# First block of a two-layer attention and MLP kernel: x and the values' weights first, constant work for TensorE meanwhile, values ahead of the folding

## The chip, the cores and the metric

The kernel runs on one core of a Trainium2 chip. The metric is device time in microseconds (us); the runs before the change gave a median of 1380.86. A core has TensorE (PE in the profile, its weight loads PEld), VectorE (DVE), ScalarE (ACT), GpSimd (POOL) and SyncE (SP), which here issues the transfers.

## The reference

Four sub-layers, each added to its input: linear attention with a learned feature map, an MLP with Mish, and both once more with the same weights. S = 2048 rows, D = 640, H = 32 heads of 20, F = 1536, all float32.

```python
def _A_ref(x, wqkv, w_phi, wo):
    qkv = (x @ wqkv).reshape(B, S, 3, H, Dh).transpose(2, 0, 3, 1, 4)
    q, k, v = qkv[0], qkv[1], qkv[2]
    pq = jnp.einsum("bhsd,hdf->bhsf", q, w_phi)
    pk = jnp.einsum("bhsd,hdf->bhsf", k, w_phi)
    phi_q = concatenate([softmax(pq), softmax(-pq)], axis=-1)     # phi_k alike
    kv = jnp.einsum("bhsf,bhsd->bhfd", phi_k, v)
    z = jnp.einsum("bhsf->bhf", phi_k)
    num = jnp.einsum("bhqf,bhfd->bhqd", phi_q, kv)
    den = jnp.einsum("bhqf,bhf->bhq", phi_q, z)[..., None] + 1e-6
    return (num / den).transpose(0, 2, 1, 3).reshape(B, S, D) @ wo
...
x = x + _A_ref(_layernorm(x), wqkv, w_phi, wo)
x = x + _B_ref(_layernorm(x), w1, b1, w2)      # dense, Mish, dense
x = x + _A_ref(_layernorm(x), wqkv, w_phi, wo)
x = x + _B_ref(_layernorm(x), w1, b1, w2)
```

## The kernel before

The rows are worked in eight blocks of 256, each of two tiles of 128 rows (tile t of block b is rows 2p+t). Every large product is made of three float32r matmuls, high by high, high by low and low by high parts; a high part (`r1h`, `r2h`, `xth`) is a ScalarE copy, the low part (`r1l`, `r2l`, `xtl`) is VectorE's difference from it.

The feature map's matrix is folded into the query and key weights on the chip: `fold_phi` (L227) multiplies the transposed weights (`raw`, from `wqk_t`) by a block-diagonal matrix (`bd`, from `phi_bd`). It goes by ten groups, five row groups k by two column halves c, each of three float32 matmuls (six in the trace) and emptied by ScalarE (L242) and VectorE (L243). There is one folding for the queries (into `r2`) and one for the keys (into the first 640 columns of `r1`); the values' weights, split by L127 and L128, are in the next 640 columns of `r1`.

A block's x is fetched (L384), its mean and variance come from VectorE (L250, L252) and a little GpSimd work (L259, L260), the scalings are L262, ScalarE writes the normalized rows `xn` (L113, L116), TensorE transposes them (L280) and the parts are split (ScalarE L116, VectorE L286). Per tile there are then three projections (`project_half`, L344): keys, values, queries, 30 matmuls each. Keys and queries go through `features`: a ScalarE copy out of PSUM, VectorE reductions (L368), subtractions (L369 on VectorE or GpSimd, L371), an exponential, a sum (L377), a reciprocal (L378) and a GpSimd product (L379). Keys are then multiplied with the values (L416); queries are transposed on VectorE (L424) and written out.

The start, in `attend_first`: SyncE asks in written order for half of `bd`, three of the queries' raw tiles, block 0's x, the rest of `bd` and raw, and after the folding for the values' weights and the keys' raw rows. Everything else is placed on the engines by a scheduler that works from its own estimates (`tc.block(schedule_with_timeline_sim=True)`); `tc.manual_schedule` keeps the written order for the engines it names, and `tc.issue_after` holds an instruction behind another. Within a block the projections have a written order (`order`): block 0 has v0, q0, v1, k0, q1, k1, block 1 has k0, q0, k1, v0, q1, v1, the later ones k0, k1, v0, v1, q0, q1. PSUM has two double tiles `mm` and four single tiles `one`.

Of the kernel before, what the change touches and what calls it, by code (L numbers as in the profile page):

```python
# [1 line left out]

# [6 lines left out]
F32 = mybir.dt.float32  # L9
F32R = mybir.dt.float32r  # L10
AF = mybir.ActivationFunctionType
# [5 lines left out]
P = 128  # L17
# [24 lines left out]
def kernel(  # L42
# [25 lines left out]
    def one_tile():  # L68
        return psum.tile([P, 512], F32, tag="one", name="one", bufs=4)
# [13 lines left out]

    ident = const.tile([P, P], F32, name="ident")
    make_identity(nc, ident)
    b1s = const.tile([P, KF], F32, name="b1s")
    neg_half = const.tile([P, BT], F32, name="neg_half")
    nc.vector.memset(neg_half, -0.5)
# [16 lines left out]
    x1_d = dram.tile([S, D], F32, name="x1_d")  # L105
    x2_d = dram.tile([S, D], F32, name="x2_d")

    last_act = [None]

    def act(*args, **kw):  # L110

        if last_act[0] is None:
            ins = nc.scalar.activation(*args, **kw)  # L113
        else:
            with tc.issue_after(last_act[0]):
                ins = nc.scalar.activation(*args, **kw)  # L116
        last_act[0] = ins.ins


    def v_tile():  # L120
        return work.tile([P, VW], F32, tag="v", name="v", bufs=2)

    def split(hi, lo, src, stage):

        st = stage()[:, :D]
        nc.sync.dma_start(st, src)
        nc.scalar.activation(hi, st, AF.Copy)  # L127
        nc.vector.tensor_tensor(lo, st, hi.bitcast(F32), op=ALU.subtract)  # L128

# [25 lines left out]
    def r1_pair(k):  # L155
        return tuple(wts.tile([P, F], F32R, tag=f"r1{s}{k}", name=f"r1{s}{k}") for s in "hl")
# [4 lines left out]
    def r2_pair(j):  # L161
# [2 lines left out]
            return w[:, 0], w[:, 1]  # L164
        return tuple(wts.tile([P, D], F32R, tag=f"r2{s}{j}", name=f"r2{s}{j}") for s in "hl")

    def load_v_weights():

        ws = [r1_pair(k) for k in range(KD)]
        for k in range(KD):  # L170
            split(ws[k][0][:, D:2 * D], ws[k][1][:, D:2 * D], wv[k * P:(k + 1) * P, :],
                  (row_tile, row_tile, v_tile, v_tile, big_tile)[k])
        return ws

    def load_q_weights():
# [36 lines left out]
    def load_raw(which, ts=range(6)):  # L212

        raw = []
        for t in ts:
            rows = 120 if t < 5 else 40
            if t < 5:
                r = wts.tile([P, D], F32, tag=f"r2{'hl'[which]}{5 + t}", name=f"raw{which}{t}")
            else:
                r = r2_wide(10 + which, F32)[:, 0]  # L220

            n = P if t < 5 else rows
            nc.sync.dma_start(r[:n], wqk_t[which * D + t * 120:which * D + t * 120 + n, :])
            raw.append((r, rows))
        return raw

    def fold_phi(ws, bd, raw):  # L227

        pss = {}
        for k, c in ((0, 0), (1, 0), (2, 0), (3, 0), (0, 1), (1, 1), (2, 1), (3, 1), (4, 0), (4, 1)):  # L230
            if c == 0:
                mm = None if k % 2 else mm_tile()
                pss[k] = [one_tile(), one_tile()] if k % 2 else [mm[:, 0], mm[:, 1]]
            ps = pss[k][c]
            for t in range(3 * c, 3 * c + 3):
                r, rows = raw[t]
                nc.tensor.matmul(ps[:, (t % 3) * 120:(t % 3) * 120 + rows],  # L237
                                 r[:rows, k * P:(k + 1) * P], bd[:rows, t, :rows],
                                 start=True, stop=True)
            n0, n1 = (0, 360) if c == 0 else (360, D)  # L240
            hi, lo = ws[k][0][:, n0:n1], ws[k][1][:, n0:n1]
            nc.scalar.activation(hi, ps[:, :n1 - n0], AF.Copy)  # L242
            nc.vector.tensor_tensor(lo, ps[:, :n1 - n0], hi.bitcast(F32), op=ALU.subtract)  # L243


    def norm_stats(t, xt):

# [48 lines left out]
    def row_tile():  # L296
        return work.tile([P, D], F32, tag="xn", name="xn", bufs=4)

    def normed(b, xt):

        xn = [row_tile() for _ in range(BT)]
        for t in range(BT):
            act(xn[t], xt[:, t, :], AF.Identity,
                                 bias=stats[:, b, 1, t:t + 1], scale=stats[:, b, 0, t:t + 1])
        return Transposed(xn)
# [23 lines left out]
    def project(xts, t, ws, col, ps=None):  # L329

        if ps is None:
            mm = mm_tile()
            ps = [mm[:, 0], mm[:, 1], mm]
        for c in range(2):
            project_half(ps[c], xts, t, ws, col, c)
        return ps
# [45 lines left out]
    def fetch(x_src, b, xt=None):  # L382
        xt = x_tile() if xt is None else xt
        nc.sync.dma_start(xt, row_block(x_src, b))  # L384
        return xt

    def attend_first(layer, x_src, first):


        def fetch_normed(b):  # L390
            if layer:
                return load_turned(n2_d[b], [row_tile] * 3)
            xt = fetch(x_src, b)
            norm_scale(b, [norm_stats(t, xt) for t in range(BT)])
            return xt

# [32 lines left out]
                if b == NB - 1:  # L429
                    yield  # L430

        def values(xts, i, v):
            vv = v.rearrange("p (h d) -> p h d", d=DH + 1)
            act(vv[:, :, DH], ident[:, :H], AF.Copy, scale=0.0, bias=1.0)
            if i < BT:
                pv = project(xts, i, kv_ws, D, [one_tile(), one_tile()])
                for c in range(2):
                    act(vv[:, c * H // 2:(c + 1) * H // 2, :DH],
                        pv[c][:, :HC].rearrange("p (h d) -> p h d", d=DH), AF.Copy)
            else:  # L440
                pv = project(xts, i % BT, kv_ws, D)
                act(vv[:, :, :DH].rearrange("p (c h) d -> p c h d", c=2),
                    both(pv).rearrange("p c (h d) -> p c h d", d=DH), AF.Copy)
            yield

        if first is None:
            with tc.manual_schedule(engines={mybir.EngineType.SP}):
                bd = big_tile()[:120, :720].rearrange("p (t c) -> p t c", t=6)
                nc.sync.dma_start(bd[:, :3], phi_bd[:, :3])
                raw = load_raw(0, range(3))  # L450
                xt = fetch_normed(0)
                nc.sync.dma_start(bd[:, 3:], phi_bd[:, 3:])
                raw += load_raw(0, range(3, 6))
                nxt = normed(0, xt).all()
                q_ws = [r2_pair(k) for k in range(KD)]
                fold_phi(q_ws, bd, raw)
                kv_ws = load_v_weights()
                raw = load_raw(1)
            nc.sync.dma_start(mask, bass.AP(tensor=head_mask.tensor, offset=head_mask.offset,
                                            ap=[[1, 120], [120 * (DH + 1), 3]]))  # L460
        else:
            nxt, kv_ws = first
            load_k_weights(kv_ws)
            q_ws = load_q_weights()
        for b in range(NB):
            xts = nxt
            order = ("k0", "k1", "v0", "v1", "q0", "q1")
            if b == 0 and layer:
                order = ("v0", "k0", "k1", "v1", "q0", "q1")
            elif b == 0:  # L470
                order = ("v0", "q0", "v1", "k0", "q1", "k1")
            elif b == 1 and not layer:
                order = ("k0", "q0", "k1", "v0", "q1", "v1")
            elif b == NB - 1:
                order = ("k0", "k1", "v0", "v1", "q0")
            vs = [v_tile() for _ in range(BT)]
            for n, (kind, t) in enumerate(order):
                t = int(t)
                i = b * BT + t
                if b == 0 and n == (1 if layer else 3):  # L480
                    if layer == 0:
                        fold_phi(kv_ws, bd, raw)
                    kva = one_tile()
                    nc.vector.memset(kva[:, :360], 0.0)
                if b == NB - 1 and n == 3:
                    loaded = {0: load(0)}
                if b + 1 < NB:
                    if n == 0:
                        xt = fetch_normed(b + 1)
                    elif n == 2:  # L490
                        nxt = xt if layer else normed(b + 1, xt)
                    elif n > 2:
                        nxt.step()
                g = {"k": lambda: keys(xts, i, vs[t]), "q": lambda: queries(xts, i),
                     "v": lambda: values(xts, i, vs[t])}[kind]()
                next(g)
                advance()
                pending.append(g)
            if b == 1:
                if layer == 0:  # L500
                    spill_qk_weights(kv_ws, q_ws)
                o_ws = load_o_weights()
# [392 lines left out]
```

## Time and profile before

| | |
|---|---|
| median of 3 runs | 1380.86 us (1379.97 to 1382.77) |
| the profiled execution | 1381.04 us |
| its span in the trace | 1379.0 us |
| busy: PE, DVE, ACT, POOL | 99%, 78%, 42%, 32% |
| chain that ended last | PE 94%, DVE 2%, DMA 1%, issue 1% |

The page of the profile shows busy time by engine and over 40 slices of 34.5 us; the view by stages gives busy time, granted clock and transfers in stretches that one names; the timeline lists instructions with start, length and, in brackets, the idle time before them and what ended it. Matmuls overlap in the trace, so the distance between their starts is their rate. L numbers are lines of the kernel before.

### The profile page before, as it was taken

The numbers are of one execution on the slowest core, as the hardware profiler recorded it, in microseconds if no ns is written. First come the engines' busy times: TensorE is split into PE (matmuls) and PEld (weight loads), VectorE is DVE, ScalarE is ACT, GpSimd is POOL, SyncE is SP. The second block draws the span as 40 slices with busy tenths as digits, with TensorE's granted clock in tenths as the row PEclk, the third lists the DMA queues.
The fourth block names the chain that finished last, engine by engine and source line by source line (L and its number), as shares of the span: only waits on it lengthen the run. The fifth ranks groups of instructions, "written<-read, shape, count | busy, mean of one in ns | idle before, by whom it ended". The sixth has DMA issues, their size and how long they took to land.

```text
span 1379.0 us, 30804 instructions
## 1 busy us (share of the span) xinstructions
PE 1364.3 (99%) x12866; PEld 1350.7 (98%) x12866; DVE 1077.0 (78%) x1820; ACT 583.3 (42%) x971; POOL 441.0 (32%) x334
## 2 busy tenths in 40 slices
PE   7999999999999999999999999999999999999998
PEld 7999999999999999999999999999999999999998
DVE  5799977886698887788769898988668776677775
ACT  4444434222355444545454333432235444354443
POOL 1353543353322221222234434453342111111112
PEclk9999999999999999999999999999999999999999
DMA  8532433779624533344473433458965321333200
GB/s 321 173 67 62 73 54 61 211 227 316 227 68 96 115 90 62 80 116 96 117 262 74 95 59 59 70 117 274 297 239 163 77 53 45 97 96 96 77 20 19
DMA packets 350277, 169.67 MB, mean 123 GB/s; under 512 B 287098, under 2 KB 323690, under 8 KB 350138
## 3 DMA queue, kind: packets, MB, share of 16 engines
q1 hardware_dynamic: 350137, 167.72, 45.0%
q8 instruction: 100, 1.64, 0.5%
q14 instruction: 40, 0.32, 0.1%
HBM read 104.76 MB, written 62.91 MB: 122 GB/s over the span
## 4 chain that ended last, share of the span: by engine, by line
PE 94%; DVE 2%; DMA 1%; issue 1%; POOL 0%; SPq 0%; ACT 0%; DVEq 0%; POOLq 0%; ACTq 0%
PE mm L344 26%; PE one L691 24%; PE mm L733 24%; PE one L344 12%; PE mm L569 3%; PE one L280 2%; PE one L416 2%; PE mm L237 1%; DMA raw<-in_wqk_t 1%; DVE m L368 1%; PE one L237 0%; DMA v<-in_wv 0%; DVE big L371 0%; DVE r L377 0%; DMA raw<-in_wo 0%
## 5 line engine op out<-in xcount | busy, mean ns | idle before, releaser
L733 PE MATMUL mm<-r2h,ol 128*128 128x320 f32 x1280 | 305.0, 309 | 0.3 <-ACT ol L716 0.3
L717 POOL TENSOR_TENSOR ol<-big,ol 128x512 fp32r<-128x512 f32 (+1 forms) x98 | 130.4, 1330 | 483.6 <-ACT ol L716 407.4
L691 PE MATMUL one<-xtl,r1h 128*128 128x256 f32 x960 | 268.2, 279 | 0.0
L691 PE MATMUL one<-xth,r1l 128*128 128x256 f32 x960 | 268.0, 279 | 0.0
L691 PE MATMUL one<-xth,r1h 128*128 128x256 f32 x960 | 265.9, 279 | 0.0
L733 PEld LDWEIGHTS mm<-r2h,ol 128*128 128x128 f32 x1280 | 219.2, 188 | 0.6 <-ACT ol L716 0.6
L733 PE MATMUL mm<-r2l,ol 128*128 128x320 f32 x640 | 197.3, 309 | 0.0
L344 PE MATMUL mm<-r1h,xth 128*128 128x320 f32 x600 | 187.5, 312 | 0.0
L344 PE MATMUL mm<-r1h,xtl 128*128 128x320 f32 x600 | 185.8, 310 | 0.4 <-DVE xtl L286 0.4
L344 PE MATMUL mm<-r1l,xth 128*128 128x320 f32 x600 | 186.0, 310 | 0.0
L691 PEld LDWEIGHTS one<-xtl,r1h 128*128 128x128 f32 x960 | 180.4, 188 | 0.0
L691 PEld LDWEIGHTS one<-xth,r1l 128*128 128x128 f32 x960 | 180.4, 188 | 0.0
L691 PEld LDWEIGHTS one<-xth,r1h 128*128 128x128 f32 x960 | 179.6, 188 | 0.0
L706 DVE TENSOR_SCALAR big<-big 128x512 f32<-128x512 f32 (+1 forms) x98 | 56.4, 575 | 110.6 <-ACT big L704 110.4
L379 POOL TENSOR_TENSOR r<-r,r 128x1280 f32<-128x1280 f32 x32 | 76.6, 2395 | 154.3 <-DVE r L378 148.5
L733 PEld LDWEIGHTS mm<-r2l,ol 128*128 128x128 f32 x640 | 120.2, 188 | 0.0
L708 ACT ACTIVATE big<-big,two 128x512 f32<-128x512 f32 (+1 forms) x98 | 70.3, 717 | 116.0 <-DVE big L707 116.0
L704 ACT ACTIVATE big<-one,b1s 128x256 f32<-128x256 f32 x192 | 81.0, 468 | 90.1 <-PE one L691 89.6
L716 ACT ACTIVATE ol<-big 128x512 fp32r<-128x512 f32 (+1 forms) x98 | 61.0, 623 | 136.3 <-DVE big L715 136.2
L344 PEld LDWEIGHTS mm<-r1h,xth 128*128 128x128 f32 x600 | 112.7, 188 | 0.8
L344 PEld LDWEIGHTS mm<-r1h,xtl 128*128 128x128 f32 x600 | 112.7, 188 | 0.7 <-DVE xtl L286 0.6
L344 PEld LDWEIGHTS mm<-r1l,xth 128*128 128x128 f32 x600 | 112.8, 188 | 0.1
(128 smaller groups left out, 3124.0 us busy)
## 6 DMA issues: line engine op xcount, KB each, us to landing
e_d<-r SPq DMA_DIRECT2D x128, 160.0 KB, 4.0
big<-e_d SPq DMA_DIRECT2D x32, 640.0 KB, 7.3
x_d<-xt SPq DMA_DIRECT2D x23, 640.0 KB, 3.6
xt<-x_d SPq DMA_DIRECT2D x22, 640.0 KB, 4.4
n_d<-xn SPq DMA_DIRECT2D x176, 80.0 KB, 2.3
xt<-in_x SPq DMA_DIRECT2D x16, 640.0 KB, 6.8
xn<-x_d SPq DMA_DIRECT2D x28, 320.0 KB, 4.4
v<-n_d SPq DMA_DIRECT2D x30, 256.0 KB, 3.1
```

Source lines behind the costliest of these rows:

```text
L280: nc.tensor.transpose(ps[:, c, t * P:(t + 1) * P], self.rows[t][:, (c0 + c) * P:(c0 + c + 1) * P], ident)
L344: nc.tensor.matmul(ps[:, :HC], a[:, sl], r, start=(k == 0 and n == 0), stop=(k == KD - 1 and n == 2))
L379: nc.gpsimd.tensor_tensor(eg, eg, r.unsqueeze(2).to_broadcast([P, 2 * H, DH]), op=ALU.mult)
L416: nc.tensor.matmul(kva[32 * j:32 * j + DH + 1, 40 * r:40 * r + 40], v[:, (DH + 1) * h:(DH + 1) * (h + 1)], e[:, 40 * h:40 * h + 40], start ...
L569: nc.tensor.matmul(po[64 * q:64 * q + 64, c, GW * j:GW * j + w], phs[g][:n, s0:s0 + 64], kvb[:n, g, :w], start=True, stop=True)
L691: nc.tensor.matmul(ph[:, j, :], l, r, start=(n == 0), stop=(n == 3 * KD - 1))
L704: exps[0] = nc.scalar.activation(part(ta, 0)[:, j - js.start], ph[:, j, :], AF.Exp, bias=b1s[:, 2 * pr + j:2 * pr + j + 1]).ins
L706: nc.vector.tensor_scalar_min(e, e, E_CAP)
L708: nc.scalar.activation(r, n, AF.Ln, bias=two)
L716: nc.scalar.activation(ah[:, js], n, AF.Copy)
L717: nc.gpsimd.tensor_tensor(al[:, js], n, ah[:, js].bitcast(F32), op=ALU.subtract)
L733: nc.tensor.matmul(pys[t][:, c, :HC], l[:, j, sl], r, start=(f == 0 and n == 0), stop=(f == KF - 1 and n == 2))
```

## The change

A chain of 58 transposes of the identity into an unused PSUM tile is put at TensorE's head. In the first layer all five engines follow a written order up to the end of the query folding: x of block 0 and its statistics, the five transfers of the values' weights, then `bd` whole, the raw rows of the queries and of the keys, and x of block 1. The values' weights are split in turns with the transposes of block 0; the second tile's normalized rows are made on VectorE instead of ScalarE; the values of tile 0 come next, and the query folding after them. Block 1 loses its own order and takes that of the later blocks. The fetch and the statistics of block 2 are held behind the last instruction of the key folding.

```diff
+    warm = one_tile()
+    for _ in range(58):
+        nc.tensor.transpose(warm[:, :P], ident, ident)
...
+    @contextmanager
+    def written():
+        in_written[0] = True
+        with tc.manual_schedule(engines={getattr(mybir.EngineType, e) for e in (
+                "PE", "SP", "Activation", "DVE", "Pool")}):
+            yield
+        in_written[0] = False
...
-            xt = fetch(x_src, b)
+            xt = fetch(x_src, b) if b > 1 else early
...
         if first is None:
-            with tc.manual_schedule(engines={mybir.EngineType.SP}):
+            with written():
+                xt = fetch(x_src, 0)
+                mvs = [norm_stats(t, xt) for t in range(BT)]
+                kv_ws = [r1_pair(k) for k in range(KD)]
+                raws = [fetch_v(k) for k in range(KD)]
                 bd = big_tile()[:120, :720].rearrange("p (t c) -> p t c", t=6)
-                nc.sync.dma_start(bd[:, :3], phi_bd[:, :3])
-                raw = load_raw(0, range(3))
-                xt = fetch_normed(0)
-                nc.sync.dma_start(bd[:, 3:], phi_bd[:, 3:])
-                raw += load_raw(0, range(3, 6))
-                nxt = normed(0, xt).all()
+                nc.sync.dma_start(bd, phi_bd)
+                raw_q = load_raw(0)
+                raw = load_raw(1)
+                early = fetch(x_src, 1)
+
+                def make_v(k):
+                    split(kv_ws[k][0][:, D:2 * D], kv_ws[k][1][:, D:2 * D], raws[k])
+
+                make_v(0)
+                norm_scale(0, mvs)
+                xn = [row_tile() for _ in range(BT)]
+                act(xn[0], xt[:, 0, :], AF.Identity, bias=stats[:, 0, 1, 0:1], scale=stats[:, 0, 0, 0:1])
+                nc.vector.tensor_scalar(xn[1], xt[:, 1, :], stats[:, 0, 0, 1:2], stats[:, 0, 1, 1:2],
+                                        op0=ALU.mult, op1=ALU.add)
+                nxt = Transposed(xn)
+                for k in range(1, KD):
+                    make_v(k)
+                    if k < 4:
+                        nxt.step()
+                vs0 = [v_tile() for _ in range(BT)]
+                pv = [one_tile(), one_tile()]
+                for k in range(KD):
+                    for c in range(2):
+                        project_half(pv[c], nxt, 0, kv_ws, D, c, range(k, k + 1))
+                next(values(nxt, 0, vs0[0], pv))
                 q_ws = [r2_pair(k) for k in range(KD)]
-                fold_phi(q_ws, bd, raw)
-                kv_ws = load_v_weights()
-                raw = load_raw(1)
+                fold_phi(q_ws, bd, raw_q)
...
-            elif b == 1 and not layer:
-                order = ("k0", "q0", "k1", "v0", "q1", "v1")
...
-                        xt = fetch_normed(b + 1)
+                        with tc.issue_after(folded[0]) if b == 1 and not layer else nullcontext():
+                            xt = fetch_normed(b + 1)
...
+                if begun and n == 0:
+                    continue
```

`folded[0]` is the last low part that a folding wrote; `begun` is block 0 of the first layer, whose first values are already under way.

More of the change, by code (lines that the diff above doesn't have):

```diff
@@ L1 @@
-from contextlib import ExitStack
+from contextlib import ExitStack, contextmanager, nullcontext
 import concourse.bass as bass
@@ L106 @@
     x2_d = dram.tile([S, D], F32, name="x2_d")
-    last_act = [None]
+    last_act, in_written = [None], [False]
+    @contextmanager
[5 more added lines that the diff above has]
+        in_written[0] = False
     def act(*args, **kw):
-        if last_act[0] is None:
+        if last_act[0] is None or in_written[0]:
             ins = nc.scalar.activation(*args, **kw)
@@ L121, in v_tile, with split @@
         return work.tile([P, VW], F32, tag="v", name="v", bufs=2)
-    def split(hi, lo, src, stage):
-        st = stage()[:, :D]
-        nc.sync.dma_start(st, src)
+    def split(hi, lo, st):
         nc.scalar.activation(hi, st, AF.Copy)
@@ L165, in r2_pair, with fetch_v @@
         return tuple(wts.tile([P, D], F32R, tag=f"r2{s}{j}", name=f"r2{s}{j}") for s in "hl")
+    def fetch_v(k):
+        st = (row_tile, row_tile, v_tile, v_tile, big_tile)[k]()[:, :D]
+        nc.sync.dma_start(st, wv[k * P:(k + 1) * P, :])
+        return st
     def load_v_weights():
@@ L170, in load_v_weights @@
         for k in range(KD):
-            split(ws[k][0][:, D:2 * D], ws[k][1][:, D:2 * D], wv[k * P:(k + 1) * P, :],
-                  (row_tile, row_tile, v_tile, v_tile, big_tile)[k])
+            split(ws[k][0][:, D:2 * D], ws[k][1][:, D:2 * D], fetch_v(k))
         return ws
@@ L242, in fold_phi @@
             nc.scalar.activation(hi, ps[:, :n1 - n0], AF.Copy)
-            nc.vector.tensor_tensor(lo, ps[:, :n1 - n0], hi.bitcast(F32), op=ALU.subtract)
+            folded[0] = nc.vector.tensor_tensor(lo, ps[:, :n1 - n0], hi.bitcast(F32), op=ALU.subtract).ins
+    folded = [None]
     def norm_stats(t, xt):
@@ L430, in queries, with values @@
                     yield
-        def values(xts, i, v):
+        def values(xts, i, v, pv=None):
             vv = v.rearrange("p (h d) -> p h d", d=DH + 1)
@@ L435, in values @@
             if i < BT:
-                pv = project(xts, i, kv_ws, D, [one_tile(), one_tile()])
+                pv = project(xts, i, kv_ws, D, [one_tile(), one_tile()]) if pv is None else pv
                 for c in range(2):
@@ L471, in attend_first @@
                 order = ("v0", "q0", "v1", "k0", "q1", "k1")
-            elif b == 1 and not layer:
-                order = ("k0", "q0", "k1", "v0", "q1", "v1")
             elif b == NB - 1:
                 order = ("k0", "k1", "v0", "v1", "q0")
-            vs = [v_tile() for _ in range(BT)]
+            begun = b == 0 and not layer
+            vs = vs0 if begun else [v_tile() for _ in range(BT)]
             for n, (kind, t) in enumerate(order):
```

## The prediction

> **What bounds the kernel now.** I read the page first, then the busy times by stage, then the timeline of the first 60 us.
>
> ```profile
> span 1379.0 us, 30804 instructions
> PE 1364.3 (99%) x12866; PEld 1350.7 (98%) x12866; DVE 1077.0 (78%) x1820; ACT 583.3 (42%) x971; POOL 441.0 (32%) x334
> PE   7999999999999999999999999999999999999998
> ```
>
> TensorE is the bound: all its slices but the first and the last are full. The change leaves its matrix work as it is (and its order from block 2 on), so only time that TensorE loses near the start can be won.
>
> ```profile
> 0.00:14.30 14.30, 6.36 (x24) 5.50 (x24) 3.18 (x13) 3.59 (x5) 1.78 (x9) 1.00 0.86 274
> 14.30:18.30 4.00, 4.00 (x20) 3.97 (x20) 4.00 (x11) 3.84 (x9) 1.47 (x3) 1.00 1.04 397
> 18.30:30.00 11.70, 11.70 (x81) 11.08 (x81) 8.52 (x22) 4.93 (x13) 1.61 (x4) 1.00 1.03 399
> 90.00:100.00 10.00, 9.58 (x182) 9.08 (x181) 10.00 (x13) 3.57 (x5) 7.53 (x6) 1.00 0.22 35
> ```
>
> Columns: busy us and count of PE, PEld, DVE, ACT and POOL, then granted clock, DMA share, GB/s. TensorE is idle 8 us of the first 14.3, then runs, but slowly: 20 instructions in 4 us against 81 in 11.7. The clock column says 1.00 throughout; the lengths say otherwise:
>
> ```profile
> L280 PE MATMUL one<-ident,xn x10: 421/421/472, 14.3 to 17.6; 128*128 128x128 f32 x10
> 16.29 1.70 PE L280 MATMUL one<-ident,xn 128*128 128x128 f32 x7
> 42.18 1.31 PE L280 MATMUL one<-ident,xn 128*128 128x128 f32 x10
> ```
>
> The same transpose takes 421 ns early, one starting every (1.70-0.42)/6 = 0.213 us. Ten later ones start every 0.115 us ((1.31-0.27)/9). TensorE becomes fast at about 18.3. The waits at the start are these:
>
> ```profile
> 0.72 0.46 SPq L449 DMA_DIRECT2D big<-in_phi_bd  x1
> 0.99 0.29 POOL masks.py:199 TENSOR_SCALAR_AFFINE_SELECT ident<-ident 128x128 f32<-128x128 f32 x1
> 1.23 1.31 SPq L223 DMA_DIRECT2D raw<-in_wqk_t  x3
> 2.58 0.43 SPq L384 DMA_DIRECT2D xt<-in_x  x1
> 4.42 1.18 PE L237 MATMUL mm<-big,raw 120*128 120x120 f32 x4 [4.42 <-DMA raw<-in_wqk_t]
> 9.54 1.67 DVE L250 BATCH_NORM_STATS2 bn<-xt 128x6 f32<-128x320 f32 x4
> 11.13 0.33 DVE L252 BATCH_NORM_AGGREGATE mv<-bn 128x2 f32<-128x12 f32 x2
> 11.96 0.71 POOL L260 TENSOR_TENSOR stats<-ve,neg_half 128x2 f32<-128x2 f32 x1
> 12.89 0.92 ACT L113 ACTIVATE xn<-xt,stats 128x640 f32<-128x640 f32 x1 [3.90 <-DVE stats L262]
> ```
>
> x is asked for fifth, behind the folding's first inputs, and is there at 9.54; its normalized rows are ready at 13.8.
>
> **The change part by part.** My mark is the end of the first key projection (block 0, tile 0). By then both versions have done the same TensorE work, the constant turns aside. It ends about 0.2 us before ScalarE copies it out, so at 49.8 before:
>
> ```profile
> 50.01 0.71 ACT L116 ACTIVATE big<-mm 128x640 f32<-128x640 f32 x1 [2.29 <-PE mm L344]
> 50.75 1.55 DVE L368 TENSOR_REDUCE m<-big 128x32 f32<-128x640 f32 x2 [2.55 <-ACT big L116]
> ```
>
> *x first.* Asked for at 0.72 (SyncE's first issue in both versions). Lower end of its landing: the first raw rows took 4.42-1.23 = 3.2 us with 0.50 MB asked for (120x360 and 128x640 in f32), x is 0.15 MB more (128x1280), at 274 GB/s, so 0.72+3.2+0.6 = 4.5. Upper end: as long as x took before, 0.72+6.96 = 7.7. I take 5.5, nearer the lower end, as nothing is queued ahead. Normalized rows came 13.81-9.54 = 4.3 us behind x; the second row now goes to DVE beside ScalarE. So they are ready at 9.8 (8.8 to 12.0).
>
> *58 constant turns.* They begin when the identity is written, 1.3, and TensorE takes work in order, so the real transposes stand behind them. All slow they end at 1.3+58*0.213 = 13.7; all fast at 8.0. Before, the clock rose 4.0 us after the gapless run from 14.3 began, or 7.1 after TensorE's run from 11.2. At 1.3+4.0 = 5.3, 19 are done and 39 fast ones remain: end 9.8. At 8.4, 33 are done: end 11.3. I start the real transposes at 10.3.
>
> *Values before the folding.* The written order makes DVE alternate the weights' low parts and the transposes' low parts:
>
> ```profile
> 42.88 0.60 ACT L116 ACTIVATE xth<-one 128x512 fp32r<-128x512 f32 x1 [0.18 <-PE one L280]
> 19.02 0.68 DVE L286 TENSOR_TENSOR xtl<-one,xth 128x512 fp32r<-128x512 f32 x1
> 19.62 0.81 DVE L128 TENSOR_TENSOR r1l<-v,r1h 128x640 fp32r<-128x640 f32 x1
> 58.64 0.41 DVE L286 TENSOR_TENSOR xtl<-one,xth 128x256 fp32r<-128x256 f32 x1
> 109.02 4.40 PE mm L344 x30
> ```
>
> From the first real transpose: 0.7 to ScalarE's copy, 0.6 copy, then on DVE 0.68+0.81+0.68+0.81+0.41+0.81 = 4.2, then the last five matmuls at 4.40/30 = 0.147, 0.7; 6.3 with hand-overs. TensorE waits beneath this chain. The values' weights land below it: five of 0.33 MB behind x, at 274 GB/s every 1.2 us, so at 6.7 to 11.5, against uses from 6.7 to 14. The first values end at 10.3+6.3 = 16.6 (16.1 by the earlier clock, 17.6 by the later).
>
> *The folding and the rest up to the mark.*
>
> ```profile
> 35.86 0.66 PE mm L237 x6
> 40.30 1.95 PE mm L237 x12
> ```
>
> Each folding has five groups at 0.66 and five at 1.95/2 = 0.975: 8.2; two make 16.4, all fast now (before, about a quarter was slow). Second values, first queries and first keys: 3*4.4 = 13.2. Transposes of block 1: 1.15. Sum 30.8. The wanted transfers lie ahead of their use: everything asked for up to block 2's x was in at 24.7, and the second folding's rows are used after 33:
>
> ```profile
> 24.74 1.67 DVE L250 BATCH_NORM_STATS2 bn<-xt 128x6 f32<-128x320 f32 x4 [0.31 <-DMA xt<-in_x]
> ```
>
> One new wait: in the built order the second folding now stands directly behind the first queries, where before 28 value matmuls lay between. ScalarE's queue there is
>
> ```profile
> 31.79 0.71 ACT L116 ACTIVATE r<-mm 128x640 f32<-128x640 f32 x1 [2.79 <-PE mm L344]
> 32.40 1.73 ACT L116 ACTIVATE xn<-xt,stats 128x640 f32<-128x640 f32 x2
> 34.15 0.42 ACT L116 ACTIVATE v<-one 128x320 f32<-128x320 f32 x1
> 34.47 0.72 ACT L148 ACTIVATE r2h<-raw 128x640 fp32r<-128x640 f32 x1
> 36.56 0.47 ACT L242 ACTIVATE r1h<-mm 128x360 fp32r<-128x360 f32 x1 [0.23 <-PE mm L237]
> 37.06 0.53 DVE L243 TENSOR_TENSOR r1l<-mm,r1h 128x360 fp32r<-128x360 f32 x1 [1.50 <-ACT r1h L242]
> ```
>
> and the second half of group 0, fifth in that folding (0.66*3+0.975*2 = 3.9 us behind), waits for group 0's first half to be emptied: 0.3+0.71+1.73+0.42+0.42+0.72+0.47+0.53 = 5.3, less overlaps of some 0.4. TensorE stalls 1.0 (0 to 1.4). So the mark comes 31.8 after the first values, at 48.4: 1.4 earlier.
>
> *Block 1 in the later order, block 2's statistics behind the folding.* VectorE has no idle time from 80 to 100, and before this cost TensorE once:
>
> ```profile
> 90.95 0.35 DVE L286 TENSOR_TENSOR xtl<-one,xth 128x256 fp32r<-128x256 f32 x1
> PE mm L344 <- DVE xtl L286: 0.4, 1, 0.4
> ```
>
> Until that third low part VectorE needed 91.3-50.75 = 40.5 us from its first key reduction, TensorE 41.3 from the mark. The new order takes one query tile's share out of this stretch (two reductions 1.55, a subtraction 0.8, a reciprocal 0.5) and adds scalings of two blocks: 39 us (37.5 to 41). But the statistics of blocks 2 and 3, twice 1.67, now stand just ahead of it, behind the folding's last low part (1.5 before the mark, 46.9): it starts at 50.5. It ends at 89.5, TensorE asks at 89.7: the 0.4 goes, with nothing to spare. Gain 1.8 in all.
>
> From block 2 on each engine has the same order, so the lead is kept to the end. The profiled execution took 1381.04 (span 1379.0), 0.18 above the median 1380.86: 1381.0-1.8 = 1379.2.
>
> **The rivals.** Write V for the end of the first values; time = 1381.0-(18.4-V).
>
> *Slower: constant turns don't raise the clock.* Then the real transposes start at 13.7, and the values run at 0.147*0.213/0.115 = 0.27. They start at 15.3 and take 8.1 all slow, V = 23.4; with the clock up 4.5 us into them 17 are slow and 13 fast, V = 21.7: 1384.3. It decides as soon as V passes 18.4. Against it: ten of the 20 instructions in 14.3 to 18.3, at whose end the clock rose, are transposes, and the run of foldings from 11.2 to 14.0 had not raised it. [...] 0.15.
>
> *No gain: the clock rises late or VectorE becomes the bound.* V = 17.6, or VectorE needs 41 us and holds TensorE 1.8 at 90: 1380.2 to 1381.5. For it: VectorE's full slices. 0.17.
>
> *More gain: ScalarE's queue costs nothing and the clock rises early.* Up after 3 us, the turns end at 9.4 (14 slow, 44 fast), with x there at 4.5: V = 15.7, and the 1.0 goes: 1377.3. For it: the stall is a sum of eight lengths whose overlap I only estimate. 0.15.
>
> **How the numbers follow.** The forecast, 1379.2 (own range 1378.0 to 1380.2), has 0.53. Over 0.2% is 2.8 us, about what a measurement can tell: below 1378.1 or above 1383.6. Faster: the third rival and the forecast's lower edge, 0.2. Slower: the first rival and a little for a clock that falls back between turns and values, 0.18. The rest 0.62. The range leaves out the first rival and the tail below 1376.6; its upper end, 1383.2, adds a stall of 2 us to the no-gain case.
>
> **What would show it.** Right: the constant turns end near 10, the first normalization statistics begin near 5.5, 30 value matmuls end near 16.6, the first key copy begins near 48.6 instead of 50.0, and the wait for the third low part near 90 is gone. Wrong: turns at 0.213 up to 13.7; a wait over 1.5 us in the second folding; a VectorE wait near 90 that has grown; or a lead at 100 us that is not there at the end.

## The result: 5 us slower, and the profile after

The changed kernel takes 1387.38 us (median of 7 executions, 1385.07 to 1389.33) against 1382.17 of the kernel before (7, 1379.97 to 1383.9): ratio 1.0036, 95% interval 1.0025 to 1.0047. Measured again later it was 1387.15 against 1381.78, ratio 1.0040 (1.0025 to 1.0055). The forecast was 1379.2.

The page of the changed kernel: span, busy times, and TensorE's 40 slices.

```profile
span 1385.1 us, 30922 instructions
PE 1369.7 (99%) x12924; PEld 1355.5 (98%) x12924; DVE 1084.3 (78%) x1821; ACT 583.2 (42%) x970; POOL 440.6 (32%) x334
PE   9989999999999999999999999999999999999998
```

The first slice is full now, and the third is not any more: what was idle at the start has moved to between 70 and 104 us. This profiled execution took 1386.9.

The start, from the timeline: the turns, the statistics of x, the real transposes, the copy of the first values, the first copy of keys.

```profile
1.34 9.35 PE L89 MATMUL one<-ident 128*128 128x128 f32 x58 [1.34 <-POOL ident masks.py:199]
4.50 0.89 DVE L267 BATCH_NORM_STATS2 bn<-xt 128x6 f32<-128x320 f32 x2 [3.62 <-DMA xt<-in_x]
10.53 1.26 PE L297 MATMUL one<-ident,xn 128*128 128x128 f32 x10
16.52 0.88 ACT L126 ACTIVATE v<-one 128x320 f32<-128x320 f32 x2 [1.95 <-PE one L361]
48.75 0.71 ACT L129 ACTIVATE big<-mm 128x640 f32<-128x640 f32 x1 [2.29 <-PE mm L361]
```

The start goes as forecast. The first key copy comes at 48.75 instead of 50.01: a lead of 1.26. What follows takes it back. The busy times by stage, in the columns of the prediction, of the kernel before:

```profile
48.60:60.00 11.40, 11.40 (x80) 11.40 (x79) 8.49 (x11) 5.65 (x9) 5.71 (x4) 1.00 0.46 149
60.00:95.00 35.00, 34.58 (x413) 33.73 (x412) 35.00 (x42) 16.32 (x23) 20.64 (x13) 1.00 0.35 70
```

And of the changed kernel:

```profile
48.60:60.00 11.40, 11.40 (x80) 11.40 (x79) 11.40 (x21) 6.66 (x10) 8.01 (x10) 1.00 0.37 119
60.00:95.00 35.00, 30.36 (x382) 29.14 (x381) 34.12 (x41) 13.32 (x19) 17.64 (x12) 1.00 0.34 70
```

VectorE has 21 instructions in 48.6 to 60 where it had 11 and is never idle there; TensorE then loses 4.6 of the 35 us up to 95, where before it lost 0.4. TensorE's waits from 60 to 110 (us in total, times, longest):

```profile
PE one L433 <- POOL big L396: 2.4, 2, 1.8
PE mm L361 <- ACT v L129: 2.2, 2, 1.3
```

The four stops in the timeline:

```profile
73.51 0.83 PE L433 MATMUL one<-big,v 128*21 128x40 f32 x64 [0.60 <-POOL big L396]
79.08 0.41 PE L361 MATMUL mm<-r2h,xth 128*128 128x320 f32 x1 [1.29 <-ACT v L129]
85.57 0.83 PE L433 MATMUL one<-big,v 128*21 128x40 f32 x64 [1.83 <-POOL big L396]
87.33 0.41 PE L361 MATMUL mm<-r2h,xth 128*128 128x320 f32 x1 [0.92 <-ACT v L129]
```

TensorE waits for GpSimd's last key product and for ScalarE's copy of the values; the wait for the third low part, on which the forecast turned, is gone. (From one start to the next the four stops take 5.7; the expectations below use that figure.) What lies behind them, from the timelines of VectorE, GpSimd and ScalarE:

```profile
46.86 1.66 DVE L267 BATCH_NORM_STATS2 bn<-xt 128x6 f32<-128x320 f32 x4
48.69 1.65 DVE L267 BATCH_NORM_STATS2 bn<-xt 128x6 f32<-128x320 f32 x4
50.26 1.52 DVE L385 TENSOR_REDUCE m<-big 128x32 f32<-128x640 f32 x2
51.82 1.58 DVE L279 SCALAR_TENSOR_TENSOR stats<-mv,stats 128x1 f32<-128x1 f32 x2
59.15 2.39 DVE L279 SCALAR_TENSOR_TENSOR stats<-mv,stats 128x1 f32<-128x1 f32 x2
67.17 1.50 DVE L441 STREAM_TRANSPOSE r<-r 128x1280 f32<-128x1280 f32 x1
70.70 2.76 POOL L396 TENSOR_TENSOR big<-big,r 128x1280 f32<-128x1280 f32 x1 [7.71 <-DVE r L395]
77.58 0.74 ACT L158 ACTIVATE r2h<-xn 128x640 fp32r<-128x640 f32 x1 [3.35 <-DMA xn<-in_wo]
78.34 0.68 ACT L129 ACTIVATE v<-mm 128x640 f32<-128x640 f32 x1
82.58 2.94 POOL L396 TENSOR_TENSOR big<-big,r 128x1280 f32<-128x1280 f32 x1
86.45 0.27 ACT L129 ACTIVATE v<-ident 128x32 f32<-128x32 f32 x1 [5.78 <-PE one L433]
88.16 2.38 DVE L279 SCALAR_TENSOR_TENSOR stats<-mv,stats 128x1 f32<-128x1 f32 x2 [0.88 <-POOL stats L277]
93.91 0.41 DVE L303 TENSOR_TENSOR xtl<-one,xth 128x256 fp32r<-128x256 f32 x1
```

Read from the top: the statistics of blocks 2 and 3 and their scalings put 1.66 + 1.65 + 1.58 + 2.39 = 7.3 us on VectorE between 46.9 and 61.5. Query 0's transposition there (67.17) is 7.4 us later than in the kernel before:

```profile
59.81 1.51 DVE L424 STREAM_TRANSPOSE r<-r 128x1280 f32<-128x1280 f32 x1 [0.76 <-POOL r L379]
```

GpSimd waits 7.71 for a reciprocal before its first key product; the value copy at 78.34 stands on ScalarE behind a copy of output weights, which SyncE had asked for only behind query 0's writes; the next one at 86.45 waits until the late key product has freed a value tile.

As a second mark I use the sixth row of key-value products of the timeline, at which both versions have done the same matrix work. Before:

```profile
152.22 1.48 PE L416 MATMUL one<-big,v 128*21 128x40 f32 x128
```

After:

```profile
155.57 1.48 PE L433 MATMUL one<-big,v 128*21 128x40 f32 x128
```

So this execution is 3.35 us behind there: between the two marks it lost 3.35 + 1.26 = 4.6 us against the kernel before, about what the four stops cost. What is missing to the 5.2 us of the medians is the subject of the last experiment.

### The profile page after: what moved, and what is told of

Read it like the earlier page. It is cut to its first block, busy times and chain, and to the rows that moved or that the text cites. A ratio compares the mean times of both kernels' runs of the same rounds, so it can differ in the third digit from the quotient of the medians.

```text
span 1385.1 us, 30922 instructions
## 1 busy us (share of the span) xinstructions
PE 1369.7 (99%) x12924; PEld 1355.5 (98%) x12924; DVE 1084.3 (78%) x1821; ACT 583.2 (42%) x970; POOL 440.6 (32%) x334
## 3 DMA queue, kind: packets, MB, share of 16 engines
q8 instruction: 101, 1.65, 0.5%
## 5 line engine op out<-in xcount | busy, mean ns | idle before, releaser
L744 ACT ACTIVATE big<-one,b1s 128x256 f32<-128x256 f32 x192 | 81.0, 468 | 89.5 <-PE one L731 88.9
```

Of the source, the lines that this page charges most:

```text
L744: exps[0] = nc.scalar.activation(part(ta, 0)[:, j - js.start], ph[:, j, :], AF.Exp, bias=b1s[:, 2 * pr + j:2 * pr + j + 1]).ins
```

## The experiments

Times are medians, with the ratio to the kernel before in the same measurement and its 95% interval. "Key copy" and "products" are the two marks, read from the one profiled execution of each version (50.01 and 152.22 before, 48.75 and 155.57 after).

| version | us | ratio | key copy | products |
|---|---|---|---|---|
| block 1 in the old order | 1387.56 | 1.0040 (1.0027 to 1.0052) | 48.84 | 158.28 |
| nothing held | 1383.02 | 1.0008 (1.0000 to 1.0017) | 50.16 | 152.36 |
| new start alone | 1384.68 | 1.0020 (1.0011 to 1.0029) | 51.93 | 155.53 |
| later order alone, on before | 1382.84 | 1.0007 (0.9997 to 1.0016) | 49.19 | 151.90 |
| block 3 held instead of 2 | 1382.76 | 1.0002 (0.9993 to 1.0011) | 52.11 | 154.82 |
| rows early | 1384.91 | 1.0019 (1.0010 to 1.0028) | 46.64 | 153.45 |
| block 3 held, rows early | 1379.64 | 0.9979 (0.9971 to 0.9988) | 47.55 | 149.70 |
| the same, block 1 in the old order | 1379.13 | 0.9977 (0.9968 to 0.9986) | 48.14 | 150.21 |
| the same as last but one, 1 turn | 1381.21 | 0.9995 (0.9986 to 1.0003) | 49.27 | 151.98 |
| changed kernel, 1 turn | 1385.60 | 1.0024 (1.0014 to 1.0034) | 51.81 | 156.99 |
| output-weight copy later | 1385.32 | 1.0027 (1.0017 to 1.0036) | 48.74 | 154.59 |

**Theory 1: the order of block 1 is the cost. Theory 2: the statistics held behind the folding are.** First the order undone:

```diff
+            elif b == 1 and not layer:
+                order = ("k0", "q0", "k1", "v0", "q1", "v1")
```

> The changed kernel with one part undone: block 1's tiles are projected in the old order (k0 q0 k1 v0 q1 v1) instead of that of the later blocks; the early values, the constant turns and block 2's held statistics stay. Theory 1 (the order of block 1 is the cost: TensorE stopped at 73.5, 79.1, 85.6 and 87.3 us, 5.7 us in sum, on GpSimd's products and ScalarE's value copies): these four stops go, TensorE loses at most 1.5 us between 60 and 95, and the time is 1382 to 1383.5 against 1387.4 of the changed kernel. Theory 2 (block 2's statistics, 3.3 us of VectorE held behind the folding, make everything behind it late): at least 3 us of stops stay between 60 and 95, and the time is 1386 to 1387.4.

1387.56: nothing comes back, theory 1 falls. The stops only change their place: ScalarE's copy of the queries behind the second one waits until query 0's rows are written out. And here something is seen that neither theory had. The two stops in the timeline:

```profile
73.56 0.83 PE L433 MATMUL one<-big,v 128*21 128x40 f32 x64 [2.77 <-POOL big L396]
76.54 0.64 PE L361 MATMUL mm<-r1h,xth 128*128 128x320 f32 x1 [2.14 <-ACT r L129]
76.97 0.47 PE L361 MATMUL mm<-r1l,xth 128*128 128x320 f32 x1
77.24 0.47 PE L361 MATMUL mm<-r1h,xtl 128*128 128x320 f32 x1
```

And the busy times just behind them, with the granted clock third from the end:

```profile
77.00:80.40 3.40, 3.40 (x14) 3.40 (x14) 3.40 (x4) 3.40 (x5) 1.78 (x2) 0.50 0.10 15
```

Behind 2.77 and 2.14 us of idle time the granted clock reads 0.50, and matrix instructions start every 0.27 us instead of 0.146.

Then the hold undone:

```diff
-                        with tc.issue_after(folded[0]) if b == 1 and not layer else nullcontext():
+                        with nullcontext():
```

> The changed kernel with the other part undone: block 2's rows and their statistics are no longer held behind the second folding; block 1 keeps the later order. Theory 1 (order): the stops on GpSimd's products and on the value copies stay within 1 us of the 5.7 us of the changed kernel, time 1386.4 to 1387.6. Theory 2 (held statistics): the key reductions start at about 47.5 instead of 50.26, VectorE is about 3 us earlier all through block 1, the stops shrink below 2.5 us, time 1383.5 to 1384.5.

1383.02: 4 us come back, as theory 2 has it; query 0's transposition starts at 60.14 instead of 67.17, and the stops of block 1 shrink to one of 0.6. But it is not under before, although it has all of the new start. The timeline says why:

```profile
25.82 1.28 DVE L267 BATCH_NORM_STATS2 bn<-xt 128x6 f32<-128x320 f32 x3
41.43 1.67 DVE L267 BATCH_NORM_STATS2 bn<-xt 128x6 f32<-128x320 f32 x4 [0.49 <-DMA xt<-in_x]
43.51 0.93 PE L252 MATMUL mm<-big,raw 120*128 120x120 f32 x6 [1.47 <-DVE r1l L258]
```

Block 2's statistics now lie at 25.8, in VectorE's idle time, and cost nothing. Block 3's have moved up into the second folding, wait there for their x, and hold up a low part that TensorE needs; so the key reductions start at 50.9, not at the expected 47.5: the path by which theory 2 was to win is not the one seen here.

Both undone, and the order alone on the kernel before (the two added lines above):

> Both of the above undone: only the new start (x and the values' weights first, constant turns, values before the folding) is left. Both theories: the 1.26 us that the new start had gained at the first key projection is kept and the stops of block 1 are gone, so 1380.4 to 1381.4, 0.8 to 1.8 under the kernel before. Against both (the new start itself is late by what it does to ScalarE's and SyncE's queues: the fifth part of the output weights lands behind query 0's writes at 77 us): 1383 or more.

> The kernel before with one part of the change alone: block 1 in the order of the later blocks. Theory 1 (order): it loses what the changed kernel loses in block 1, 3 to 5 us, 1385.2 to 1387.2 against 1382.2, with stops on GpSimd's products between 60 and 95. Theory 2 (held statistics): VectorE has the statistics early here, so the order alone costs less than 1 us: 1381.5 to 1383.

The new start alone is slower than before, 1384.68, against both theories' 1380.4 to 1381.4; "1383 or more" had been the third case. It has the same stop in the folding, of 1.6 us, behind it the granted clock at 0.50 from 45.0 to 48.4, and in block 1 one stop of 1.7. So without the hold the old order is the slower one (1384.68 against 1383.02, with intervals that overlap a little). The later order alone moves nothing that can be told from no change.

**Repairs.** If what stands behind and inside the folding decides, the hold belongs on block 3 instead of block 2; and the 1.0 us that the forecast laid to ScalarE's queue goes if block 1's rows are normalized one step earlier:

```diff
-                        with tc.issue_after(folded[0]) if b == 1 and not layer else nullcontext():
+                        with tc.issue_after(folded[0]) if b == 2 and not layer else nullcontext():
...
-                    elif n == 2:
+                    if n == (1 if b == 0 and not layer else 2):
                         nxt = xt if layer else normed(b + 1, xt)
```

The first edit alone, the second alone, and both:

> The changed kernel with the hold moved by one block: block 2's statistics go free (VectorE takes them at 25.8, where it is idle), block 3's stand behind the second folding. Theory 2 (what stands behind the folding on VectorE decides, at 1.65 us a block): the stop of 1.75 us that the kernel without any hold showed inside the folding at 43.5 goes, the key reductions start at 48.5 to 49 instead of 50.26, the stops of block 1 stay under 1.5 us: 1380.3 to 1381.8, a little under the kernel before. Theory 1 (any wait behind the folding tips block 1 over): stops of 3 us or more come back between 60 and 95: 1385 or more.

> The changed kernel with one thing added: block 1's rows are normalized one step earlier, so that their 1.73 us of ScalarE come before the second folding instead of inside it; the hold stays. If the 1.0 us stop at 39.4 (and the 0.35 at 37.5) is ScalarE's queue as forecast, both go and the first key projection ends 1.0 to 1.4 us earlier; TensorE then waits as much longer in block 1, where the held statistics still decide: 1385.5 to 1387.4. If the stop is something else, nothing moves at 39.4.

> Both together: the hold on block 3 instead of block 2, and block 1's rows normalized one step earlier. If the two costs are separate they add: another 1.0 to 1.4 us under the version with the moved hold, 1379.0 to 1380.7, and under the kernel before. If what is won inside the folding is lost again in block 1, it is the same as the version with the moved hold.

Both together give 1379.64, 0.21% under the kernel before. The two costs about add: 0.0034 and 0.0017 taken from 1.0036 would leave a ratio of 0.9985, measured is 0.9979. The one wait of TensorE that is left from 30 to 110 in the repaired version:

```profile
PE mm L361 <- ACT v L129: 0.6, 1, 0.6
```

Its first key copy and the products in the timeline:

```profile
47.55 0.69 ACT L129 ACTIVATE big<-mm 128x640 f32<-128x640 f32 x1
149.70 1.47 PE L433 MATMUL one<-big,v 128*21 128x40 f32 x128
```

And the stage that had lost 4.6 us:

```profile
60.00:95.00 35.00, 34.45 (x468) 33.17 (x467) 32.96 (x40) 14.58 (x20) 18.03 (x11) 1.00 0.34 70
```

In the version with the early rows alone, no wait of TensorE is left in the second folding: its 0.83 was ScalarE's queue, as forecast. Its first key copy comes at 46.64, but block 1 has the stops on GpSimd and the value copies as before (2.4 and 2.2 us), and it is 1384.91 against an expected 1385.5 to 1387.4. With the hold moved alone, block 1 keeps one stop of 0.9, but 1382.76 is above the expected 1380.3 to 1381.8, and its key reductions start at 52.8, not at 48.5 to 49: the folding is where it stays behind. Busy times there:

```profile
41.50:44.90 3.40, 3.40 (x17) 3.11 (x16) 1.14 (x3) 0.53 (x2) 0.00 (x0) 0.50 1.01 395
44.90:48.30 3.40, 3.40 (x15) 3.40 (x15) 0.53 (x1) 0.47 (x1) 1.55 (x1) 0.51 0.81 313
```

And of the changed kernel's first profile:

```profile
41.50:44.90 3.40, 3.40 (x27) 3.35 (x27) 1.58 (x3) 1.07 (x3) 1.58 (x1) 1.00 1.03 392
```

Behind two short stops at 38.8 and 40.1 (0.6 and 0.9 from start to start) the clock is at half for 6.8 us.

**The order and the turns, on the repaired version.** The old order again (the two added lines), and 1 turn instead of 58; the latter also on the changed kernel itself:

> The version with both repairs with block 1's projections in the old order again. If the later order is worth something once the statistics are out of the way: 1 to 2.5 us more than with the later order, 1380.6 to 1382.2, with a stop over 1 us between 60 and 95. If the order is worth nothing (the order alone on the kernel before gave no gain, 1382.8 against 1381.7): within 0.7 us, 1379 to 1380.3.

> The version with both repairs (hold on block 3, block 1's rows normalized early; 1379.64 against 1382.54 of the kernel before) with 1 constant turn instead of 58. Where nothing behind eats it, the turns are worth what the first values showed: without them these ended at 18.0 instead of 15.7 to 16.8, so 1.3 to 2.3 us more, 1381 to 1382. If the turns only moved a wait: within 0.5 us of the version with them.

```diff
-    for _ in range(58):
+    for _ in range(1):
```

> The changed kernel with 1 constant turn instead of 58, nothing else touched. If the 58 turns raised the clock (its record rises at 7.1 us with them, at 18.3 in the kernel before): the real transposes start earlier, at about 9.6, but run at 0.213 us each, the value matmuls slowly behind them until the clock rises some 7 us later; the first values end near 18.7 instead of 16.8 and the first key projection is 1.5 to 2.5 us later. If the turns did nothing: the transposes start at 9.6 instead of 10.5 and the first key projection is up to 0.9 us earlier. The time itself follows only in part, since VectorE's lateness behind the folding sets block 1: 1387 to 1389.5 in the first case, 1386.5 to 1387.5 in the second.

In the repaired version the order is worth nothing either way: 0.9977 and 0.9979. The turns are worth 1.6 us by the medians (1381.21 against 1379.64), 2.2 by the ratios. On the changed kernel the transposes without them run slowly again, and the first values are copied 1.3 us later:

```profile
9.70 2.39 PE L297 MATMUL one<-ident,xn 128*128 128x128 f32 x10 [7.88 <-ACT xn L126]
17.80 0.88 ACT L126 ACTIVATE v<-one 128x320 f32<-128x320 f32 x2 [3.56 <-PE one L361]
```

The key copy came 3.1 later, not 1.5 to 2.5, since the granted clock was at 0.50 once more in the folding (43.1 to 46.5). Yet this version took 1385.60, less than the changed kernel, against the expected 1387 to 1389.5; the intervals of the ratios overlap, and why the later start doesn't cost more in block 1 is open.

**How VectorE's lateness reaches TensorE.**

```diff
-            make_parts(w, raws[k], low=low)
+            make_parts(w, raws[k], ordered=(k == 4 and j == KD), low=low)
```

> The changed kernel with one instruction moved: ScalarE's copy of the fifth part of the output weights, which had waited until 77.6 for its rows with block 1's value copy queued behind it, stands behind block 1's value copies. If that copy passes the lateness on (the rows are asked for behind query 0's writes, which stand behind query 0's transposition, 7.4 us late): the stop of 1.56 us at 79.1 goes, that of 2.1 us at 85.6 shrinks to under 1, time 1384 to 1386. If VectorE's lateness reaches TensorE by the keys' products alone: the stops at 73.5, 85.6 and 87.3 stay, only the 1.56 shrinks, time 1386 to 1387.4.

1385.32, inside the first theory's 1384 to 1386, but only half as it said: the value copy comes at 74.5 and the stop at 79 is gone, that at 85.6 is 1.1 from start to start instead of 2.1, the one at 87.3 stays, and two new ones of 0.8 and 0.9 appear at 89.9 and 93.8, behind GpSimd's product and VectorE's low part. So the output-weight copy carries a part (the products come 1.0 earlier), and without it VectorE's lateness finds TensorE directly.

**Where the rest of the 5 us is.** The changed kernel itself, five times more:

> The changed kernel once more, as it is: its profile lost 2.2 us more than that of the kernel before between 700 and 1016 us, in single waits at 711, 934 and 1015 us behind transfers, though each engine has the same order there. If these are chance meetings of one execution, the wait at 1015 us is gone or the sum of the three is under 1 us more than before, and the stops of block 1 (5.7 us in sum between 60 and 95) are there again. If they follow from the later start of the blocks, the three are there again with 2 us or more. Time 1386.5 to 1388 either way.

> One more execution of the changed kernel with its profile, the first of four. Its executions spread from 1384.3 to 1391.2, and the two seen in profile (1384.3 and 1386.9) lost the same up to 95 us. If the clock decides (behind TensorE's stops at 85 and 87 us its matrix instructions start every 0.267 us instead of 0.146 for some microseconds in some executions, as was seen behind the 3.1 us stop of the version with block 1's old order): executions above 1386.5 show such a stretch, worth 1.5 to 3 us, those below 1385 none. If it is the waits behind transfers at 711, 934 and 1015 us: no such stretch, and the slow executions lose 2 us or more between 690 and 1020 us.

> The second of the four executions, with the same expectations: above 1386.5 either a stretch of slow matrix instructions behind block 1's stops (clock) or 2 us more lost between 690 and 1020 us (transfers).

> The third of the four executions, with the same expectations: above 1386.5 either a stretch of slow matrix instructions behind block 1's stops (clock) or 2 us more lost between 690 and 1020 us (transfers).

> The fourth of the four executions, with the same expectations: above 1386.5 either a stretch of slow matrix instructions behind block 1's stops (clock) or 2 us more lost between 690 and 1020 us (transfers).

| execution | us | key copy | products | granted clock at 0.50 |
|---|---|---|---|---|
| first profile | 1386.90 | 48.75 | 155.57 | none |
| again | 1384.26 | 48.53 | 155.34 | none |
| first of the four | 1392.28 | 52.46 | 161.73 | 38.6 to 48.8, 89.8 to 96.6 |
| second | 1389.79 | 51.60 | 160.87 | 40.8 to 47.6, 88.6 to 95.4 |
| third | 1388.18 | 49.67 | 158.74 | 40.0 to 43.4, 87.8 to 91.2 |
| fourth | 1388.05 | 48.70 | 157.96 | 85.6 to 92.4 |

The last column is read between 30 and 100 us. All four of these executions above 1388 show the clock at half behind block 1's stops, three of them also in the second folding. Busy times of the first of the four just behind the stop at 89 to 91, and in the folding:

```profile
91.30:94.70 3.40, 3.40 (x14) 3.40 (x14) 2.98 (x3) 2.07 (x4) 2.71 (x2) 0.50 0.70 106
41.50:44.90 3.40, 3.40 (x16) 3.11 (x16) 1.14 (x2) 0.83 (x2) 0.00 (x0) 0.50 1.02 391
```

Of the fourth, just behind the stop:

```profile
87.90:91.30 3.40, 3.40 (x14) 3.40 (x14) 3.35 (x3) 2.07 (x4) 2.34 (x2) 0.50 0.58 92
```

And of the first profile at the same place, where the clock stays:

```profile
87.70:91.10 3.40, 3.40 (x25) 3.40 (x24) 2.94 (x3) 2.09 (x4) 2.76 (x2) 1.00 0.71 108
```

14 matrix instructions instead of 25. From products to end the six executions take 1228.9 to 1231.3, before 1228.8. Of the first profile's 2.4 us more than the repeat's, 2.2 are waits at 934, 937 and 1015 us (0.8, 0.3 and 1.1) that the repeat does not have; that at 711 is in both. The wait at 1015 stands behind a transfer of x, so transfers explain some of the scatter; what lies behind the other two was not followed. But up to the products the six differ by 6.4, and most of that is the time at half clock. The mean granted clock that every execution lists says the same: 0.999 or 1.000 in 85 of 87 executions of the kernel before, in 2 of 17 of the changed kernel, and in all 20 of the two repaired versions with 58 turns. The repeat, without a stretch at half clock, is 2.5 us above the median of the kernel before measured with it (1384.26 against 1381.78): about half of what the changed kernel loses is there without the clock, and the rest comes in executions in which the clock fell.

## Why the prediction was wrong, step by step

**x first, turns, values: right.** x was there at 4.50 (forecast 5.5), the turns ended at 10.7 (9.8 to 11.3), the transposes started at 10.53 (10.3), and the first values were copied at 16.5 (16.6). The rival that constant turns don't raise the clock is refuted: 58 of them at 0.213 would take 12.4 us and took 9.35, from 7.5 us on each half us has 7 of them in work where from 2.0 to 7.0 it had 4 or 5, and without them the first values come 1.3 later.

**The stall of 1.0 in the second folding: right in place, size and cause** (0.83 of waiting, 1.1 from start to start; gone when the rows are normalized earlier), and the mark came at 48.75 where 48.6 was forecast. Its price was not: in three of six executions the clock fell behind it, and the key copy came 0.9 to 3.7 us later still.

**The VectorE step failed.** It has VectorE start at 50.5 (50.26), need 39 us (37.5 to 41) and end the third low part at 89.5; it ended at 94.3, after 44.1. The term that was mis-sized is the scalings. What the step takes out of 40.5 (2.85) leaves some 1.35 for them in its 39. They are 128x1 instructions, a pair of which took 0.23 us at 27.21, where GpSimd is idle, but the two pairs that were counted took 1.58 and 2.39, and a third, not counted, fell into the stretch (2.38 at 88.16): 6.35 in sum, 5.0 more than the sum had, against 5.1 that VectorE was late. This is read from the trace; no run moved the scalings alone. The kernel before could have shown it: its pair at 44.12 takes 1.61, beside a GpSimd instruction of 1.58 at 44.07. And the step asked the wrong question: whether VectorE reaches one low part in time. What ended last were the products and copies that hang on its results in between, GpSimd's key product, query 0's writes, the output weights behind them and the value copies; I had costed only VectorE's own total, with nothing to spare, and called that no cost. The statistics of block 2 had a place at 25.8 to 29.6 at no price; the hold took them out of it.

**The rivals.** "VectorE becomes the bound" had the right engine with 0.17, but held TensorE for 1.8 at most; the stops are 4.6. The slower side was given to the turns, which work; the rises of the clock at 3 us and at 4.5 us into the values that two rivals count with were my estimates, and with the turns the starts quicken at about 7 us, 5.7 behind the first turn. What made most of the profiled executions slower still, a stop behind which the granted clock fell to 0.50, stood only as "a clock that falls back between turns and values".

**"The lead is kept to the end": right within the scatter.** From the products on the executions of the changed kernel differ from the kernel before by 2.5 us at most, and the repeat by 0.1. The lead of 1.26 was lost before 95 us, not on the way to the end.

What stays open: what decides in an execution whether the clock falls behind these stops, and why one turn costs the changed kernel nothing in its median.

## What to carry to other kernels

Where an engine off the critical path is full, ask of each step moved onto it not whether its total fits, but which results leave it on the way and who waits for each; and look first for the idle stretch in which the step stood. A stop of TensorE cost here its own length and, in a part of the executions, more at half clock behind it (0.9 to 3.7 us behind the one in the second folding, in three of six), so short stops close together are worth removing before long preparations at the start. One profile of a version whose executions spread is not enough to price it: read several, or the mean clock of all.

## What the hardware showed that I had not expected

**The clock fell behind stops of 0.6 to 2.8 us.** Two stops of 0.6 and 0.9 in sparse foldings were followed by 6.8 us at 0.50; with stops of 2.77 and 2.14 the clock fell inside the second, also for 6.8 (75.6 to 82.4). Read in slices of 0.2 us, each stretch at 0.50 between 30 and 100 us lasts 3.4, 6.8 or 10.2, and within one execution two falls lie a multiple of 3.41 apart: 38.6 and 89.8 (51.2, 15 times), 40.8 and 88.6, 40.0 and 87.8 (47.8, 14 times). In the 3.41 us ahead of each of the eleven falls that the profiles show there TensorE is busy for only 0.7 to 2.6 us. That alone does not decide it: in the changed kernel's first profile TensorE is busy for 0.83 of the 3.41 us up to 87.33, and the granted clock stays at 1.00. The wait of 0.83 in the second folding, too, has a fall behind it in the first and the second of the four executions and none in the first profile. What decides, no run shows.

**Two pairs of VectorE scalings ended with GpSimd's instruction.** A pair of 128x1 scalings, from the timeline, next to GpSimd's work at that time:

```profile
27.21 0.23 DVE L279 SCALAR_TENSOR_TENSOR stats<-mv,stats 128x1 f32<-128x1 f32 x2 [0.50 <-POOL stats L277]
58.52 2.93 POOL L396 TENSOR_TENSOR r<-r,r 128x1280 f32<-128x1280 f32 x1
```

The pair at 27.21 took 0.23, with GpSimd idle from 27.17 on. The pair at 59.15 took 2.39 and ended at 61.54, GpSimd's product at 61.45; the pair at 51.82 took 1.58 and ended at 53.40, GpSimd's subtraction beside it at 53.39:

```profile
51.81 1.58 POOL L159 TENSOR_TENSOR r2l<-raw,r2h 128x640 fp32r<-128x640 f32 x1 [1.85 <-ACT r2h L158]
```

Each time the pair ends within 0.1 us of the end of the GpSimd instruction during which it began.
